# Modulation columns and k weights in blocks of 128 rows at the beginning of an adaLN block

## The chip, the cores and the metric

The kernel runs on one core of a Trainium2 chip. The metric is the device time of one execution in microseconds (us), the median of several runs. A profile of one execution shows when each engine worked: TensorE (PE, with its weight loads as PEld), VectorE (DVE), ScalarE (ACT), GpSimd (POOL) and the queue of SyncE (SP), which issues the transfers.

## What is computed

```python
x = A_x                                            # 2048 x 512, all float32
sa, ca, ga, sb, cb, gb = silu(c) @ w_mod           # six vectors of 512
h = layernorm(x) * (1 + ca) + sa
x = x + ga * linear_attention(h, wqkv, wo)         # 32 heads of 16
h = layernorm(x) * (1 + cb) + sb
x = x + gb * (((h @ w_gate) * (h @ w_up)) @ w_down)
```

The linear attention uses phi(t) = t + 1 above zero and exp(t) below, plus 1e-6, for q and k. Its first sum runs over all 2048 tokens, phi(k) against v, so k of all tokens comes before any output. Products are made in three passes from a high and a low part of each operand (float32r), so one k tile of 128 tokens is four blocks of 128 rows times three matmuls, 12 in all.

## The kernel before

The 2048 tokens are four chunks of four tiles; a tile is 128 tokens by 512 features. The schedule is written out by hand: each engine runs its instructions in the order of the program text, and waits only for data and for buffers. SyncE takes the loads in the order of the text too; a queue of some eight loads is in flight at a time. SBUF tiles come from one pool of 99 buffers, PSUM tiles from two pools of four banks (acc_bank and bank).

At the beginning SyncE loads (lines 122 to 132) the first chunk of x, the vector c, the 512 columns of w_mod for ca as four tiles of 128 x 512, the same for sa, the four row blocks of the k weights, the second chunk of x, the q and v weights and the rest of x.

The work of the beginning (lines 343 to 389) is then:

- keep_on puts filler matmuls on TensorE that keep it busy until data is there. stats, rstd_of, nmr_of and xhat normalise the four tiles of the first chunk (statistics on DVE, a power on POOL, the normalisation on ACT), and transpose_token turns them on TensorE, so that bank k holds 128 features of 512 tokens.
- silu gives the vector sc. mod_acc adds up, on DVE, the four tiles of w_mod, each times a column of sc (lines 159 and 161). mod_col (line 166) adds the result over its 128 partitions on TensorE with a matmul of one moving column for each block of 128 features, and col_out (line 171) brings the column to SBUF. This is done for ca in full, then for sa in full.
- split_raw makes the high part of a weight block on ACT (line 183) and the low part on DVE (line 184). modulated (lines 262 to 273) applies scale and shift to one block of 128 features on ACT, then makes the high part (a cast on DVE with cast, or on ACT) and the low part on DVE.
- product2 (lines 206 to 208) makes k of tiles 0 and 1 block by block; tiles 2 and 3 follow by proj (lines 196 to 198). In between nx, the norm of the second chunk, has its statistics (line 225), variance (233), power (234), nmr (237) and first normalisations (243); k_phi makes phi(k) with two ACT operations and one DVE operation (291, 292, 295), k_split its parts (318, 319).

Behind that stands the loop over 16 tiles. Its first turn makes k of tile 3, normalises the third and the fourth tile of chunk 1 (with k_split_x of tile 1 between them on ACT), runs two of the four column groups of t_tile(0) on TensorE (lines 327 to 329), and then transposes chunk 1 (line 250). The rest of the kernel, with attention and the feed-forward part (line 837 has most of its matmuls), follows that loop.

Of the kernel before, what the change touches and what calls it, by code (L numbers as in the profile page):

```python
# [8 lines left out]
F32 = mybir.dt.float32  # L9
F32R = mybir.dt.float32r  # L10
AF = mybir.ActivationFunctionType
ALU = mybir.AluOpType
AX = mybir.AxisListType

P = 128
# [7 lines left out]
def tile_adaln_block(  # L23
# [12 lines left out]
    nc = tc.nc  # L36
    ctx.enter_context(tc.manual_schedule())
    _, S, D = x.shape
    F = w_gate.shape[1]
    KD = D // P  # L40
# [12 lines left out]
    wqkv_v = wqkv.rearrange("(k p) n -> k p n", p=P)  # L53
# [3 lines left out]
    wm_v = w_mod.rearrange("(p k) n -> p k n", k=KD)  # L57

    pool = lambda name, bufs, **kw: ctx.enter_context(tc.tile_pool(name=name, bufs=bufs, **kw))
    consts = pool("consts", 1)  # L60
# [5 lines left out]
    def f32(ap):  # L66
        return ap.bitcast(F32)
# [3 lines left out]
    def T(p, tag, shape=(P, D), dt=F32, bufs=None):  # L71
        cnt[0] += 1
        return p.tile(list(shape), dt, tag="t" if p is tiles else tag, name=f"{tag}_{cnt[0]}", bufs=bufs)

    def B(tag, shape=(P, D), dt=F32):

        return T(tiles, tag, shape, dt)

    def acc_bank():
        return T(ps_acc, "acc")  # L80

    def bank():
        return T(ps_w, "bank")
# [24 lines left out]
    def load(src, tag):  # L108
        raw = B(tag, (P, *src.shape[1:]))[:src.shape[0]]
        nc.sync.dma_start(raw, src)  # L110
        return raw

    def load_x(ch):
        return [load(xv[ch, j], "x") for j in range(NJ)]

    def load_mod(v):
        return [load(wm_v[:, k, v * D:(v + 1) * D], "raw") for k in range(KD)]

    def load_qkv(n):
        return [load(wqkv_v[k, :, n * D:(n + 1) * D], "raw") for k in range(KD)]  # L120
# [1 line left out]
    xts = [load_x(0)]  # L122
    ct = consts.tile([P, KD], F32, name="ct")
    nc.sync.dma_start(ct, c[0].rearrange("(p k) -> p k", k=KD))
    raw_ca = load_mod(1)
    raw_sa = load_mod(0)
    raw_k = load_qkv(1)
    xts.append(load_x(1))
    raw_q = load_qkv(0)
    raw_v = load_qkv(2)  # L130
# [10 lines left out]
    def keep_on(n):  # L141
        for _ in range(n):
            nc.tensor.matmul(ps_idle, idle[:, :P], idle, start=True, stop=True)
# [3 lines left out]
    sc = consts.tile([P, KD], F32, name="sc")  # L147
# [8 lines left out]
    def mod_acc(acc, raws, ks):  # L156
        for k in ks:
            if k == 0:
                nc.vector.tensor_scalar(acc, raws[k], sc[:, 0:1], None, op0=ALU.mult)
            else:  # L160
                nc.vector.scalar_tensor_tensor(acc, raws[k], sc[:, k:k + 1], acc, op0=ALU.mult, op1=ALU.add)

    def mod_col(acc, ps):

        for b in range(KD):
            nc.tensor.matmul(ps[:, b:b + 1], acc[:, b * P:(b + 1) * P], ones[:, 0:1], start=True, stop=True)
        return ps

    def col_out(v, ps, add):
        t = consts.tile([P, KD], F32, name=f"col{v}")  # L170
        nc.vector.tensor_scalar(t, ps[:, :KD], add, None, op0=ALU.add)
        return t
# [9 lines left out]
    def split(src, h, l, low=None):  # L182
        nc.scalar.activation(h, src, AF.Copy)  # L183
        (low or nc.vector).tensor_tensor(l, src, f32(h), op=ALU.subtract)  # L184

    def split_raw(raw, shape=(P, D), low=None):
        h = B("w", shape, F32R)
        l = B("w", shape, F32R)
        split(raw, h[:raw.shape[0]], l[:raw.shape[0]], low)
        return h, l  # L190
# [6 lines left out]
            nc.tensor.matmul(ps, ah, bl, start=False, stop=False)  # L197
            nc.tensor.matmul(ps, al, bh, start=False, stop=i == n - 1)  # L198

    def product2(pss, pairs):  # L200

        n = len(pairs[0])
        for i in range(n):
            for ps, p in zip(pss, pairs):
                (ah, al), (bh, bl) = p[i]
                nc.tensor.matmul(ps, ah, bh, start=i == 0, stop=False)
                nc.tensor.matmul(ps, ah, bl, start=False, stop=False)
                nc.tensor.matmul(ps, al, bh, start=False, stop=i == n - 1)

    def cut(pair, a, b):  # L210
        return pair[0][:, a:b], pair[1][:, a:b]


    class Norm:
# [25 lines left out]
        def xhat(self, *js):  # L240
            for j in js:
                self.n[j] = B("n")
                nc.scalar.activation(self.n[j], self.tiles[j], AF.Identity,  # L243
                                     scale=self.rstd[:, j:j + 1], bias=self.nmr[:, j:j + 1])

        def transpose(self, *ks):
            for k in ks:
# [31 lines left out]
    wk, wq, wv = [], [], []  # L279
    kx, phk, phq, q_ps = {}, {}, {}, {}  # L280

    def proj(i, w, of=bank):

        ch, j = divmod(i, NJ)
        ps = of()
        product(ps, [(cut(norm[ch].t[k], j * P, (j + 1) * P), w[k]) for k in range(KD)])
        return ps
# [9 lines left out]
    def k_split_x(i):  # L297
        ch, j = divmod(i, NJ)
        kx[i] = [B("xh", dt=F32R), B("xl", dt=F32R)]
        split(norm[ch].n[j], *kx[i])  # L300

    def k_phi(i, ps):
        phi = B("phi")
        phi_a(ps, phi)
        phi_b(ps, phi)
        phk[i] = phi
# [8 lines left out]
    def k_split(i):  # L315
        h, l = B("kh", dt=F32R), B("kl", dt=F32R)
        phi = phk[i]
        nc.scalar.activation(h, phi, AF.Identity, bias=eps_phi)
        nc.vector.scalar_tensor_tensor(l, phi, EPS_PHI, f32(h), op0=ALU.add, op1=ALU.subtract)
        kx[i] += [h, l]  # L320
# [18 lines left out]
    zacc = B("z")  # L339

    n0 = norm[0]
    acc_ca, acc_sa = B("f"), B("f")
    keep_on(20)
    n0.stats(0, 1)
    n0.rstd_of(0, 2)
    n0.stats(2, 3)
    n0.rstd_of(2, 4)
    silu()
    n0.nmr_of(0, 2)
    n0.xhat(0, 1)  # L350
    mod_acc(acc_ca, raw_ca, [0])
    n0.nmr_of(2, 4)
    n0.xhat(2, 3)
    n0.transpose_token(0)
    keep_on(2)
    n0.transpose_token(1)
    keep_on(2)
    n0.transpose_token(2)
    mod_acc(acc_ca, raw_ca, [1, 2, 3])
    keep_on(1)  # L360
    n0.transpose_token(3)
    ps_ca = mod_col(acc_ca, acc_bank())
    mod_acc(acc_sa, raw_sa, [0, 1, 2, 3])
    ca = col_out(1, ps_ca, 1.0)
    keep_on(4)
    ps_sa = mod_col(acc_sa, acc_bank())
    keep_on(9)
    wk.append(split_raw(raw_k[0]))
    sa = col_out(0, ps_sa, 0.0)
    nx = Norm(xts[1])  # L370
    nx.stats(0)
    n0.modulated(ca, sa, 0, cast=nc.vector)
    wk.append(split_raw(raw_k[1]))
    n0.modulated(ca, sa, 1, cast=nc.vector)
    wk.append(split_raw(raw_k[2]))
    n0.modulated(ca, sa, 2)
    nx.stats(1)
    wk.append(split_raw(raw_k[3]))
    n0.modulated(ca, sa, 3)
    ps0, ps1 = acc_bank(), acc_bank()  # L380
    product2((ps0, ps1), [[(cut(n0.t[k], j * P, (j + 1) * P), wk[k]) for k in range(KD)] for j in range(2)])
    nx.stats(2, 3)
    nx.rstd_of()
    k_split_x(0)
    k_phi(0, ps0)
    nx.nmr_of()
    k_phi(1, ps1)
    k_split(0)
    nx.xhat(0, 1)

    tacc = [acc_bank() for _ in range(KD)]
    rows, cols = {}, {}
    accs = {}

    raw_m, raw_o, wo_s = {}, [], []

    def mod_load(*vs):
        raw_m.update({v: load_mod(v) for v in vs})
# [18 lines left out]
             13: lambda: (mod_part(5, 0, 1, 2), cols.update({4: col_out(4, mod_col(accs[4], bank()), 1.0)})),  # L417
             14: lambda: (mod_part(5, 3), wo_s.extend(split_raw(x) for x in raw_o)), 15: lambda: rows.update({5: mod_row(5, accs[5])})}
    q_at = {3: 0, 4: 1, 6: 2, 7: 3}
    ahead = {2: proj(2, wk)}  # L420
    for i in range(NT):
        ch, j = divmod(i, NJ)
        more = ch + 1 < NCH
        if i == 0:
            ahead[3] = proj(3, wk)
        elif i > 1:
            ahead[i + 2] = proj(i + 2, wk) if i + 2 < NT else proj(i + 6 - NT, wq)
        if i in q_at:
            qps = proj(q_at[i], wq)
        if more and j == 0:  # L430
            nx.xhat(2)
        if i + 1 < NT:
            k_split_x(i + 1)
        if more and j == 0:
            nx.xhat(3)
        if i + 1 < NT:
            k_split(i + 1)
        if more and j < 2:
            t_tile(i, 0, 1)
            nx.transpose(2 * j, 2 * j + 1)  # L440
            nx.modulated(ca, sa, 2 * j, 2 * j + 1, cast=nc.vector)
            norm[ch + 1:] = [nx]
        if ch + 2 < NCH and j == 2:
            nx2 = Norm(xts[ch + 2])
            nx2.stats(0, 1)
        if ch + 2 < NCH and j == 3:
            nx = nx2
            nx.stats(2, 3)
            nx.rstd_of()
            nx.nmr_of()  # L450
            nx.xhat(0, 1)
        if i + 2 < NT:
            k_phi(i + 2, ahead.pop(i + 2))
        else:
            q_a(i + 6 - NT, ahead.pop(i + 2))
            q_b(i + 6 - NT)
        if i in q_at:
            q_a(q_at[i], qps)
            q_b(q_at[i])
        if i + 1 < NT:  # L460
            z_add(i + 1)
        if i == NT - 1:
            zps = bank()
            nc.tensor.matmul(zps, ones, zacc, start=True, stop=True)
            zb = consts.tile([P, D], F32, name="zb")
            nc.scalar.activation(zb, zps, AF.Identity, bias=eps_z)
        t_tile(i, *range(2 if more and j < 2 else 0, KD))
        if i in extra:
            extra[i]()
# [61 lines left out]
    ps = proj(6, wq)  # L531
    fs, tt = [], []
    for k in range(KD):
        f = B("n")
# [9 lines left out]
    for g in range(KD):  # L544
        a, b = g * P, (g + 1) * P
# [4 lines left out]
    ps = proj(8, wq)  # L550
# [9 lines left out]
    ps = proj(9, wq)  # L560
# [444 lines left out]
    ps = proj(11, wq)  # L1005
# [177 lines left out]
```

## Time and profile before

| What | Value |
|---|---|
| Median of 3 runs | 572.92 us (571.94 to 573.11) |
| Span of the profiled execution, first to last instruction | 570.9 us |
| TensorE busy | 560.6 us, 98% |
| VectorE busy | 373.8 us, 65% |
| ScalarE busy | 279.7 us, 49% |
| GpSimd busy | 185.6 us, 33% |
| Instructions | 7343 |

For the profiled execution the span is what is known of its own time; it is 2.0 us under the median of the runs. A row of the timeline has the start, the time it took (both in us), the engine, the line in the kernel, the operation, the tiles written and read with their shape, the count, and in brackets the idle time of the engine before it and what ended that. L166 is line 166. Matmuls overlap each other, so their distance is read from the starts. A row of the waits has who waited for whom, the total in us, how often, and the longest. A row of the stage windows has the stretch, its length, the busy time of PE, PEld, DVE, ACT and POOL, the granted TensorE clock (1.00 is full), the busy share of the DMA engines, and GB/s.

### The profile page before, as it was taken

The numbers are of one execution on the slowest core, as the hardware profiler recorded it, in microseconds if no ns is written. First come the engines' busy times: TensorE is split into PE (matmuls) and PEld (weight loads), VectorE is DVE, ScalarE is ACT, GpSimd is POOL, SyncE is SP. The second block draws the span as 40 slices with busy tenths as digits, with TensorE's granted clock in tenths as the row PEclk, the third lists the DMA queues.
The fourth block names the chain that finished last, engine by engine and source line by source line (L and its number), as shares of the span: only waits on it lengthen the run. The fifth ranks groups of instructions, "written<-read, shape, count | busy, mean of one in ns | idle before, by whom it ended". The sixth has DMA issues, their size and how long they took to land.

```text
span 570.9 us, 7343 instructions
## 1 busy us (share of the span) xinstructions
PE 560.6 (98%) x2569; PEld 457.3 (80%) x2569; DVE 373.8 (65%) x613; ACT 279.7 (49%) x500; POOL 185.6 (33%) x191
## 2 busy tenths in 40 slices
PE   7999999999999999999989999999999999999997
PEld 6778888888888778878878888887888888888885
DVE  6876868868768876768776777755554434344444
ACT  3785857546456535445865545533333333334110
POOL 2000000000011300000389666665667446556200
PEclk9999999999999999999999999999999999999999
DMA  8900223302301000804208462699436122100004
GB/s 279 378 6 2 73 75 102 121 0 57 96 0 52 24 1 37 258 0 136 68 2 276 147 209 93 218 337 335 126 110 174 29 56 55 57 18 2 0 1 147
DMA packets 50165, 59.34 MB, mean 104 GB/s; under 512 B 6416, under 2 KB 26896, under 8 KB 50128
## 3 DMA queue, kind: packets, MB, share of 16 engines
q1 hardware_dynamic: 50128, 58.87, 32.0%
q8 instruction: 20, 0.33, 0.2%
q14 instruction: 17, 0.14, 0.1%
HBM read 43.12 MB, written 15.73 MB: 103 GB/s over the span
## 4 chain that ended last, share of the span: by engine, by line
PE 88%; DVE 4%; ACT 2%; DMA 2%; POOL 2%; issue 1%; SPq 0%; POOLq 0%; DVEq 0%; ACTq 0%
PE bank L837 28%; PE acc L614 7%; PE acc L916 6%; PE acc L917 6%; PE acc L918 6%; PE bank L198 5%; PE bank L196 5%; PE bank L197 5%; PE acc L329 3%; PE acc L328 3%; PE acc L327 3%; PE bank L691 2%; PE bank L692 2%; PE bank L690 2%; PE bank L250 1%; PE bank L578 1%
## 5 line engine op out<-in xcount | busy, mean ns | idle before, releaser
L837 PE MATMUL bank<-h,w 128*128 128x512 f32 (+1 forms) x798 | 185.3, 390 | 1.6 <-DVE u L892 1.6
L837 PEld LDWEIGHTS bank<-h,w 128*128 128x128 f32 (+1 forms) x798 | 148.2, 186 | 34.9 <-DVE u L892 2.5
L842 ACT ACTIVATE bank<-bank 128x512 f32<-128x512 f32 (+1 forms) x38 | 22.2, 583 | 144.7 <-PE bank L837 144.7
L677 DVE TENSOR_TENSOR x<-acc,x 128x512 f32<-128x512 f32 x72 | 48.9, 690 | 49.2 <-PE acc L918 48.5
L823 POOL TENSOR_TENSOR w<-raw,w 128x256 fp32r<-128x256 f32 (+3 forms) x38 | 42.2, 1111 | 97.0 <-ACT w L816 76.7
L184 POOL TENSOR_TENSOR w<-raw,w 128x512 fp32r<-128x512 f32 (+1 forms) x25 | 35.5, 1422 | 115.9 <-DVE mv L226 87.5
L916 PE MATMUL acc<-w,kh 128*128 128x512 f32 (+1 forms) x152 | 59.2, 390 | 0.0
L917 PE MATMUL acc<-w,kh 128*128 128x512 f32 (+1 forms) x152 | 59.2, 390 | 0.0
L918 PE MATMUL acc<-w,kl 128*128 128x512 f32 (+1 forms) x152 | 59.1, 389 | 0.0
L234 POOL TENSOR_TENSOR rstd<-ve,half 128x4 f32<-128x4 f32 (+1 forms) x9 | 9.4, 1045 | 138.2 <-DVE ve L233 136.6
L184 DVE TENSOR_TENSOR kl<-u,kh 128x512 fp32r<-128x512 f32 (+1 forms) x38 | 27.4, 761 | 34.5 <-ACT kh L183 32.6
L823 POOL TENSOR_TENSOR w<-t,w 128x512 fp32r<-128x512 f32 (+1 forms) x38 | 48.0, 1286 | 0.0
L196 PE MATMUL bank<-w,h 128*128 128x512 f32 x112 | 44.9, 401 | 0.0
L198 PE MATMUL bank<-w,h 128*128 128x512 f32 x112 | 43.9, 392 | 0.0
L197 PE MATMUL bank<-w,h 128*128 128x512 f32 x112 | 43.6, 389 | 0.0
L614 PE MATMUL acc<-w,xh 128*128 128x512 f32 x120 | 38.1, 398 | 0.0
L916 PEld LDWEIGHTS acc<-w,kh 128*128 128x128 f32 (+1 forms) x152 | 28.5, 188 | 6.0
L918 PEld LDWEIGHTS acc<-w,kl 128*128 128x128 f32 (+1 forms) x152 | 28.5, 188 | 6.0
L917 PEld LDWEIGHTS acc<-w,kh 128*128 128x128 f32 (+1 forms) x152 | 28.5, 188 | 6.0
L243 ACT ACTIVATE n<-x,nmr,rstd 128x512 f32<-128x512 f32 x32 | 24.1, 805 | 17.2 <-DVE nmr L237 17.2
L892 DVE TENSOR_TENSOR u<-bank,u 128x512 f32<-128x512 f32 (+1 forms) x19 | 13.1, 691 | 28.8 <-PE bank L837 28.8
L183 ACT ACTIVATE w<-raw 128x512 fp32r<-128x512 f32 (+2 forms) x44 | 26.4, 618 | 3.2 <-DMA raw<-in_A_wqkv_dram 2.2
(177 smaller groups left out, 1098.1 us busy)
## 6 DMA issues: line engine op xcount, KB each, us to landing
raw<-in_w_mod_dram SPq DMA_DIRECT2D x24, 256.0 KB, 3.7
raw<-in_B_w_down_dram SPq DMA_DIRECT2D x20, 256.0 KB, 3.0
raw<-in_B_w_gate_dram SPq DMA_DIRECT2D x36, 128.0 KB, 3.5
raw<-in_B_w_up_dram SPq DMA_DIRECT2D x36, 128.0 KB, 3.6
x<-in_A_x_dram SPq DMA_DIRECT2D x16, 256.0 KB, 5.4
kept<-f SPq DMA_DIRECT2D x16, 256.0 KB, 2.1
f<-kept SPq DMA_DIRECT2D x16, 256.0 KB, 4.6
side_s<-h SPq DMA_DIRECT2D x16, 256.0 KB, 2.9
```

The source lines that it names most:

```text
L183: nc.scalar.activation(h, src, AF.Copy)
L184: (low or nc.vector).tensor_tensor(l, src, f32(h), op=ALU.subtract)
L196: nc.tensor.matmul(ps, ah, bh, start=i == 0, stop=False)
L197: nc.tensor.matmul(ps, ah, bl, start=False, stop=False)
L198: nc.tensor.matmul(ps, al, bh, start=False, stop=i == n - 1)
L614: nc.tensor.matmul(yps[i], x, y, start=False, stop=k == KD - 1 and x is al, skip_group_check=True)
L677: nc.vector.tensor_tensor(xt, dn[j], xt, op=ALU.add)
L823: sub = lambda out, x, y: (on or nc.gpsimd).tensor_tensor(out, x, f32(y), op=ALU.subtract)
L837: mm = lambda x, y, **kw: nc.tensor.matmul(ps, x[:, k], y, skip_group_check=True, **kw)
L916: nc.tensor.matmul(dn[j], hh[:, a:b], dh[:n], start=i == 0, stop=False)
L917: nc.tensor.matmul(dn[j], hh[:, a:b], dl[:n], start=False, stop=False)
L918: nc.tensor.matmul(dn[j], hl[:, a:b], dh[:n], start=False, stop=i == len(hs) - 1)
```

## The change

The loads of w_mod for ca and sa are cut by feature blocks in place of the rows: one load now has all 512 input rows of 128 columns (128 partitions x 4 x 128), and the order is ca block b, sa block b, k rows block b, for b = 0 to 3. The sums of mod_acc at the beginning are gone: mod_block(b) makes both columns of a block on TensorE from the loaded tiles, four accumulated matmuls for each, and mod_out(b) brings both to SBUF in one DVE operation. The fourth tile of the first chunk is normalised on DVE. k of the first four tiles is made in four PSUM banks, block by block between the column blocks, so that proj for tiles 2 and 3 disappears. The order of the next chunk's statistics against k_phi and k_split changes, and ten fillers go.

```diff
-    raw_ca = load_mod(1)
-    raw_sa = load_mod(0)
-    raw_k = load_qkv(1)
+    raw_m, raw_k = {}, []
+    for b in range(KD):
+        for v in (1, 0):
+            raw_m[v, b] = load(wm_v[:, :, v * D + b * P:v * D + (b + 1) * P], "raw")
+        raw_k.append(load(wqkv_v[b, :, D:2 * D], "raw"))
     xts.append(load_x(1))
...
+        def xhat_on(self, engine, *js):
+            for j in js:
+                self.n[j] = B("n")
+                engine.tensor_scalar(self.n[j], self.tiles[j], self.mv[:, j, 0:1], self.rstd[:, j:j + 1],
+                                     op0=ALU.subtract, op1=ALU.mult)
...
-    acc_ca, acc_sa = B("f"), B("f")
+    add = consts.tile([P, 2], F32, name="add")
+    nc.gpsimd.memset(add[:, 0:1], 1.0)
+    nc.gpsimd.memset(add[:, 1:2], 0.0)
+    mod = consts.tile([P, 2, KD], F32, name="mod")
+    ca, sa = mod[:, 0], mod[:, 1]
+    ps_mod = acc_bank()[:, :2 * KD].rearrange("p (v b) -> p v b", v=2)
+
+    def mod_block(b):
+        for i, v in enumerate((1, 0)):
+            raw = raw_m.pop((v, b))
+            for k in range(KD):
+                nc.tensor.matmul(ps_mod[:, i, b:b + 1], raw[:, k], sc[:, k:k + 1], start=k == 0, stop=k == KD - 1)
+
+    def mod_out(b):
+        nc.vector.tensor_tensor(mod[:, :, b], ps_mod[:, :, b], add, op=ALU.add)
+
+    def block_in(b):
+        n0.modulated(ca, sa, b, cast=nc.vector)
+
+    def w_in(b):
+        wk.append(split_raw(raw_k[b]))
+
     keep_on(20)
     n0.stats(0, 1)
     n0.rstd_of(0, 2)
-    n0.stats(2, 3)
+    n0.stats(2)
+    n0.nmr_of(0, 2)
+    n0.xhat(0)
+    n0.stats(3)
     n0.rstd_of(2, 4)
     silu()
-    n0.nmr_of(0, 2)
-    n0.xhat(0, 1)
-    mod_acc(acc_ca, raw_ca, [0])
-    n0.nmr_of(2, 4)
-    n0.xhat(2, 3)
+    n0.xhat(1)
+    n0.nmr_of(2, 3)
+    n0.xhat(2)
+    n0.xhat_on(nc.vector, 3)
     n0.transpose_token(0)
     keep_on(2)
     n0.transpose_token(1)
     keep_on(2)
+    mod_block(0)
+    n0.transpose_token(3)
     n0.transpose_token(2)
-    mod_acc(acc_ca, raw_ca, [1, 2, 3])
-    keep_on(1)
-    n0.transpose_token(3)
-    ps_ca = mod_col(acc_ca, acc_bank())
-    mod_acc(acc_sa, raw_sa, [0, 1, 2, 3])
-    ca = col_out(1, ps_ca, 1.0)
+    mod_out(0)
     keep_on(4)
-    ps_sa = mod_col(acc_sa, acc_bank())
-    keep_on(9)
-    wk.append(split_raw(raw_k[0]))
-    sa = col_out(0, ps_sa, 0.0)
+    w_in(0)
+    block_in(0)
+    k_ps = [acc_bank(), acc_bank(), bank(), bank()]
+
+    def k_block(b, *js):
+        for j in js:
+            (hh, hl), (wh, wl) = cut(n0.t[b], j * P, (j + 1) * P), wk[b]
+            nc.tensor.matmul(k_ps[j], hh, wh, start=b == 0, stop=False)
+            nc.tensor.matmul(k_ps[j], hh, wl, start=False, stop=False)
+            nc.tensor.matmul(k_ps[j], hl, wh, start=False, stop=b == KD - 1)
+
+    k_block(0, 0, 1)
+    mod_block(1)
+    w_in(1)
+    mod_out(1)
+    k_block(0, 2)
+    block_in(1)
+    k_block(0, 3)
+    k_block(1, 0, 1)
+    mod_block(2)
+    w_in(2)
+    k_split_x(0)
+    mod_out(2)
     nx = Norm(xts[1])
     nx.stats(0)
-    n0.modulated(ca, sa, 0, cast=nc.vector)
-    wk.append(split_raw(raw_k[1]))
-    n0.modulated(ca, sa, 1, cast=nc.vector)
-    wk.append(split_raw(raw_k[2]))
-    n0.modulated(ca, sa, 2)
+    k_block(1, 2)
+    mod_block(3)
+    block_in(2)
+    w_in(3)
+    mod_out(3)
+    k_block(1, 3)
+    block_in(3)
+    k_block(2, 0)
+    k_block(3, 0)
     nx.stats(1)
-    wk.append(split_raw(raw_k[3]))
-    n0.modulated(ca, sa, 3)
-    ps0, ps1 = acc_bank(), acc_bank()
-    product2((ps0, ps1), [[(cut(n0.t[k], j * P, (j + 1) * P), wk[k]) for k in range(KD)] for j in range(2)])
-    nx.stats(2, 3)
+    k_phi(0, k_ps[0])
+    k_block(2, 1)
+    k_block(3, 1)
+    nx.stats(2)
+    k_split(0)
+    k_phi(1, k_ps[1])
+    nx.stats(3)
     nx.rstd_of()
-    k_split_x(0)
-    k_phi(0, ps0)
+    k_block(2, 2, 3)
+    k_block(3, 2, 3)
     nx.nmr_of()
-    k_phi(1, ps1)
-    k_split(0)
     nx.xhat(0, 1)
...
-    ahead = {2: proj(2, wk)}
+    ahead = {2: k_ps[2], 3: k_ps[3]}
     for i in range(NT):
         ch, j = divmod(i, NJ)
         more = ch + 1 < NCH
-        if i == 0:
-            ahead[3] = proj(3, wk)
-        elif i > 1:
+        if i > 1:
```

More of the change, by code (lines that the diff above doesn't have):

```diff
@@ L198, in product @@
             nc.tensor.matmul(ps, al, bh, start=False, stop=i == n - 1)
[L200 to L208, printed above, removed]
     def cut(pair, a, b):
@@ L393, in tile_adaln_block @@
     accs = {}
-    raw_m, raw_o, wo_s = {}, [], []
+    raw_o, wo_s = [], []
     def mod_load(*vs):
```

## The prediction

> **What bounds the kernel now.** I read four views: the page for the span and the chain that ended last, the waits of TensorE over the whole span, the timeline of the first 45 us, and the stage windows for the clock and the transfers.
>
> ```profile
> span 570.9 us, 7343 instructions
> PE 88%; DVE 4%; ACT 2%; DMA 2%; POOL 2%; issue 1%; SPq 0%; POOLq 0%; DVEq 0%; ACTq 0%
> ```
>
> ```profile
> PE bank L257 <- ACT n L243: 1.6, 1, 1.6
> PE bank L837 <- DVE u L892: 1.6, 2, 1.5
> ```
>
> The chain is TensorE for 88% of the span. The longest waits of its matmuls once data is in are 1.6 us in total each, one of them at the very beginning (L257, the first transposes) and one in the last part (L837). So whatever moves TensorE's steady work later or earlier at the beginning moves the end by about the same amount: nothing behind it is idle enough to absorb it. The change touches only the beginning, so I look at when TensorE gets into its steady sequence. The mark I use is the first transposes of the second chunk (L250), because everything behind them has the same order before and after.
>
> ```profile
> 16.37 0.78 ACT L262 ACTIVATE f<-bank,col,col 128x512 f32<-128x512 f32 x1 [1.25 <-DVE col L171]
> ...
> 18.47 0.50 PE L206 MATMUL acc<-w,h 128*128 128x512 f32 x1 [0.18 <-DVE h L270]
> ...
> 24.08 0.50 PE L208 MATMUL acc<-w,h 128*128 128x512 f32 x1
> ...
> 24.62 0.60 ACT L291 ACTIVATE phi<-acc 128x512 f32<-128x512 f32 x1 [2.04 <-PE acc L208]
> 25.25 0.63 ACT L292 ACTIVATE phi<-phi 128x512 f32<-128x512 f32 x1
> 25.67 0.17 DVE L233 TENSOR_SCALAR ve<-mv 128x4 f32<-128x4 f32 x1
> 25.92 1.38 POOL L234 TENSOR_TENSOR rstd<-ve,half 128x4 f32<-128x4 f32 x1 [16.11 <-DVE ve L233]
> 26.35 0.68 DVE L295 SCALAR_TENSOR_TENSOR phi<-acc,phi 128x512 f32<-128x512 f32 x1
> 27.07 0.72 ACT L318 ACTIVATE kh<-phi,eps_phi 128x512 fp32r<-128x512 f32 x1
> 27.70 2.21 ACT L243 ACTIVATE n<-x,nmr,rstd 128x512 f32<-128x512 f32 x3
> 29.82 0.62 ACT L183 ACTIVATE xh<-n 128x512 fp32r<-128x512 f32 x1
> 30.34 0.80 ACT L243 ACTIVATE n<-x,nmr,rstd 128x512 f32<-128x512 f32 x1
> ```
>
> ```profile
> 30.60 0.39 PE L327 MATMUL acc<-kh,xh 128*128 128x512 f32 x1
> ...
> 31.96 1.04 PE L250 MATMUL bank<-ident,n 128*128 128x128 f32 x8
> ```
>
> The reader is to see two strands that meet at 31.96. One is TensorE: the first k tile complete at 24.58, two more products, six matmuls of L327 to L329 from 30.60 (1.36 us, 0.227 each), then the transposes. The other is the second chunk's norm: its variance line L233 at 25.67, the power on POOL, and four normalisations on ACT, the last over at 31.14. It is 0.8 us early, so it costs nothing. It is early because L233 stands **ahead** of the k features on DVE: 25.67 against 26.35 for the first of them.
>
> **The change part by part.** The columns first. Each goes from sums on DVE and one reduction per column to four accumulated products per column, eight in a block of 128 rows. The nearest row is the reduction itself, the same shapes, 128x128 weights and one moving column:
>
> ```profile
> 13.20 0.95 PE L166 MATMUL acc<-ones,f 128*128 128x1 f32 x8
> ```
>
> Four calls are eight passes in 0.95 us, of which the last ends 0.25 late: 0.10 us a pass. mod_block is eight calls, sixteen passes, 1.66 us; four blocks are 6.6 us of TensorE in place of 1.9 for both columns. As bounds I take half of that pass (0.05) and one and a half (0.15). [...]
>
> What this buys is DVE: eight operations of L159 and L161 go. The transfers:
>
> ```profile
> 7.66 0.70 DVE L225 BATCH_NORM_STATS2 st<-x 128x6 f32<-128x512 f32 x1 [0.39 <-DMA x<-in_A_x_dram]
> ```
>
> ```profile
> 10.00:11.00 1.00, 0.77 (x6) 0.73 (x7) 0.96 (x3) 1.00 (x3) 0.00 (x0) 1.00 1.07 412
> ```
>
> ```profile
> 140.00:142.00 2.00, 2.00 (x20) 1.96 (x18) 1.63 (x4) 1.09 (x2) 0.00 (x0) 1.00 1.03 292
> ```
>
> ```profile
> raw<-in_B_w_gate_dram SPq DMA_DIRECT2D x2, 256.0 KB, 3.9
> ```
>
> The new w_mod loads have rows of 512 bytes, as the w_gate loads at 140 us: 292 GB/s in place of 412 (the last number of a window row), 0.9 us a load in place of some 0.65. From the fourth tile of x at 7.66 on: columns of block 0 at about 10.0, its k rows at 10.6, and so on every 2.4 us; block 3's columns at 17.3, its k rows at 18.0. SP issues as many DMAs as before in the same place, and the second chunk of x slips by some 1.5 us, to 18.6 to 20.7. All of this turns out early against what follows, so the transfers cost nothing, and the cover is 6 us in block 3.
>
> Now the queues, each instruction at the later of its engine's turn and its inputs, and some 0.05 us from one engine to the next (24.58 to 24.62 above).
>
> ```profile
> 2.00 6.60 PE L143 MATMUL acc<-w 128*128 128x512 f32 x20 [2.00 <-DVE w L138]
> 6.58 0.71 POOL L234 TENSOR_TENSOR rstd<-ve,half 128x2 f32<-128x2 f32 x1 [3.91 <-DVE ve L233]
> ...
> 11.19 0.60 PE L257 MATMUL bank<-ident,n 128*128 128x128 f32 x4
> 12.09 0.60 PE L257 MATMUL bank<-ident,n 128*128 128x128 f32 x4
> ...
> 18.02 0.40 DVE L270 CAST h<-f 128x512 fp32r<-128x512 f32 x1
> 18.45 0.69 DVE L273 TENSOR_TENSOR h<-f,h 128x512 fp32r<-128x512 f32 x1
> ...
> 24.76 0.66 DVE L225 BATCH_NORM_STATS2 st<-x 128x6 f32<-128x512 f32 x1
> 25.45 0.18 DVE L226 BATCH_NORM_AGGREGATE mv<-st 128x2 f32<-128x6 f32 x1
> ```
>
> *Start.* The first rstd is there at 7.29, so xhat(0) starts at 7.45. The fillers end at 8.60; two groups of transposes with two fillers each, 0.95 a group by the starts of L257, bring TensorE to 10.5. xhat on DVE for the fourth token is bounded by nothing and by the 0.80 that ACT takes for the same tile; even with that it is over by 10.8, ahead of its transposes, so it costs nothing. The two new memsets on POOL fall into its idle time before L234 (3.91 us). mod_block(0) runs 10.5 to 12.2, two groups of transposes to 13.0, the modulated tile f0 on ACT 13.0 to 13.8 (0.78), the cast 0.42: first k product at 14.3 in place of 18.47. That is the gain.
>
> *Blocks 0 to 2.* Six products to 15.95 (with 0.3 waiting for the low part). Behind them mod_block(1), whose loads landed long ago, to 17.6; only then can mod_out(1), f1 (18.0 to 18.8) and the next cast run. This wait of DVE on mod_out is new, and behind it in DVE's queue stand the next cast, its low part and the split's low part, for which TensorE then waits. Tile 3's product waits 0.55 for the bank that f1 reads; block 1's six products end at 20.95, mod_block(2) at 22.6, three products, mod_block(3) at 24.95. On DVE mod_out(3) stands behind statistics of the next chunk, h2, its low part and a split, and comes at 25.5; f3 25.7 to 26.5, cast 27.0, low part 27.7. **Tile 0 is complete at 28.2**, against 24.58: three blocks' 5.0 us of columns and a round trip TensorE, DVE, ACT, DVE for each take back the early start.
>
> ```profile
> 50.95 1.01 POOL L234 TENSOR_TENSOR rstd<-ve,half 128x4 f32<-128x4 f32 x1 [23.65 <-DVE ve L233]
> ```
>
> *Behind tile 0.* The last statistics of the next chunk, with L233, now stand **behind** k_phi(1) on DVE. From 28.2: Relu 0.62, Exp 0.68, phi 0.73 (tile 0); kh 0.63; Relu 0.62, Exp 0.68, phi 0.60 (tile 1); statistics 0.92; variance 0.22; the power 1.25 (its two rows have 1.38 and 1.01); nmr 0.21, like the variance; three normalisations at 0.70, a copy 0.53, the fourth 0.83: 10.7 us with the 0.05 that lead in. Transposes at **38.8**, against 31.96: 6.9 late.
>
> TensorE meanwhile has 18 products and 6 matmuls of the first t tile, 24 at 0.227, and is through at about 33.5. It waits 5.3 us, and all that is behind the transposes waits with it. The same arithmetic on the order of before gives 31.9 where the row has 31.96.
>
> *The clock.* What such a wait costs beside itself:
>
> ```profile
> 566.44 0.39 PE L918 MATMUL acc<-w,kl 128*128 128x512 f32 x1
> ```
>
> ```profile
> 568.00:569.00 1.00, 0.00 (x0) 0.00 (x0) 0.00 (x0) 0.00 (x0) 0.00 (x0) 1.00 0.57 217
> 569.00:570.00 1.00, 0.00 (x0) 0.00 (x0) 0.00 (x0) 0.00 (x0) 0.00 (x0) 0.53 0.12 45
> ```
>
> After the last matmul (over at 566.83) the granted clock, the third number from the end, falls to half within the slice from 569.0: by its mean 0.53 at about 569.1, after 2.2 us. So a wait of 5.3 us should bring half clock. Coming back is shown by the first 20 fillers: 6.60 us where 20 at 0.227 would take 4.7, a loss of 1.9. Some of it falls into a stall that is there anyway:
>
> ```profile
> 39.22 0.40 PE L196 MATMUL bank<-w,h 128*128 128x512 f32 x1
> ...
> 41.15 0.40 PE L327 MATMUL acc<-kh,xh 128*128 128x512 f32 x1
> ```
>
> Six products in 1.93 where 1.36 would do: 0.6 to spare. I add 1.2 (bounds 0 and 2.1). [...]
>
> **The sum** is 6.9 + 1.2 = 8.1 us on the profiled span of 570.9, so 579.0. The median of the runs is 572.92, 2.0 above the span; with the same 2.0 the forecast is 581.0. By half the price of a pass (0.05) the sum is 2.5 smaller, by one and a half (0.15) 2.5 larger.
>
> **The rivals.** *The clock holds* through the wait, as it did through the 1.6 us of L257: 572.9 + 6.9 = 579.8. [...] *The clock falls earlier*, between 10 and 26 us, because a pass moves one column and counts as little work: another 1.9 us of lost speed on the path, about 583; against it, TensorE is never idle for more than 0.7 us there, and the gap of 1.6 us at L257 did no harm. *The other side:* tile 0's path doesn't run through the column passes, because they fall into TensorE's waits and the loads set the pace. Then block 3 ends with its columns at 17.3, mod_out, f3, cast and low part 2.6 later, tile 0 complete at 20.4, transposes 10.7 behind it at 31.1: 0.9 earlier, 572.0. It decides from 21.3 on (31.96 less 10.7); the queue order, with mod_block(b) behind products that wait for block b-1's tile, speaks against it, and even passes that cost nothing leave the round trips (tile 0 at 23.8, 2.6 slower). *The change doesn't do what it says:* transfers in rows of 512 bytes so slow that every block waits for its columns; that needs 1.6 us a load in place of 0.9, and would add to the loss.
>
> **How the numbers follow.** Forecast 0.60; clock holds 0.20; cheap passes 0.06; earlier fall 0.07; the other side 0.05; slow transfers 0.02. The range takes in the clock case, cheap passes down to 0.06 and the upper bounds of clock and passes in part: 578.0 to 583.5. About 0.2% (1.1 us) is what a measurement can tell from no change. Faster by more than that 0.04, within it 0.03, slower 0.93, since only the other side and what I have not seen lie below.
>
> **What would show it.** In the changed profile: L166's successor passes at 0.10 us; first k product near 14.3; idle time of ACT and DVE ended by column passes; tile 0's Relu near 28.2; variance L233 near 33.7; the transposes L250 near 38.8 with some 5 us of TensorE idle before them, released by ACT n; granted clock near 0.5 behind them for some 4 us. I am wrong if tile 0 is complete before 21.3, or if L233 runs ahead of the k features.

## The result, and the profile after

The changed kernel takes **582.27 us** (580.95 to 583.34, five runs), beside 571.98 us (571.85 to 573.11, five runs) for the kernel before: a ratio of 1.0175, interval 1.0161 to 1.019. It is slower, as forecast, and inside the range; the forecast of 581.0 is 1.3 low. The profiled execution has a span of 580.1 us where the one before had 570.9: 9.2 more, against 8.1 in the sum. The medians are 10.3 apart, since the two profiled executions are not the median ones: 580.1 is 0.5 under the median span of the changed kernel (580.6), and 570.9 is some 0.6 above that of the kernel before (its median time less the 1.7 that lies between time and span in the runs that list both). What follows explains the 9.2.

The timeline of the changed kernel shows the steps of the prediction. L351 are the column passes, L354 mod_out, L391 to L393 the k products, L260 modulated, L289 the Relu of phi, L225 to L229 the second chunk's variance, power and nmr, L235 its normalisation, L248 its transposes (the old L250), L325 to L327 t_tile.

```profile
10.84 1.84 PE L351 MATMUL acc<-sc,raw 128*128 128x1 f32 x16
...
14.62 0.51 PE L391 MATMUL acc<-w,h 128*128 128x512 f32 x1
...
16.36 1.84 PE L351 MATMUL acc<-sc,raw 128*128 128x1 f32 x16
...
18.24 0.16 DVE L354 TENSOR_TENSOR mod<-acc,add 128x2 f32<-128x2 f32 x1 [2.35 <-PE acc L351]
18.44 0.78 ACT L260 ACTIVATE f<-bank,mod 128x512 f32<-128x512 f32 x1 [3.81 <-DVE mod L354]
...
28.80 0.60 ACT L289 ACTIVATE phi<-acc 128x512 f32<-128x512 f32 x1 [1.78 <-PE acc L393]
...
33.84 0.39 PE L327 MATMUL acc<-kl,xh 128*128 128x512 f32 x1
...
34.27 0.17 DVE L225 TENSOR_SCALAR ve<-mv 128x4 f32<-128x4 f32 x1
...
35.76 2.22 ACT L235 ACTIVATE n<-x,nmr,rstd 128x512 f32<-128x512 f32 x3 [3.07 <-DVE nmr L229]
36.62 0.33 PE L248 MATMUL bank<-ident,n 128*128 128x128 f32 x1 [2.39 <-ACT n L235]
...
39.26 1.33 PE L248 MATMUL bank<-ident,n 128*128 128x128 f32 x5 [0.75 <-ACT n L235]
...
40.24 0.78 PE L325 MATMUL acc<-kh,xh 128*128 128x512 f32 x1
```

The reader is to see the two delays one behind the other. The first product is early (14.62, before 18.47), but each further block waits for its columns: DVE for TensorE (2.35 us), then ACT for DVE (3.81 us). Tile 0 is complete at 28.76 in place of 24.58. Then the second chunk's variance, now queued behind the k features, comes at 34.27 in place of 25.67; TensorE has run out of matmuls at 34.23, and its idle time is ended by ACT's normalised tiles. The waits of 8 to 50 us say the same in four rows (who waits for whom, total, how often, longest):

```profile
ACT f L260 <- DVE mod L354: 8.5, 3, 3.8
DVE mod L354 <- PE acc L351: 6.8, 3, 2.7
ACT n L235 <- DVE nmr L229: 5.7, 3, 3.1
...
PE bank L248 <- ACT n L235: 3.9, 4, 2.4
```

The stage windows of the same execution show the clock (third number from the end) and the rate of the transfers (last number):

```profile
14.00:16.00 2.00, 1.93 (x8) 0.98 (x7) 1.72 (x3) 0.63 (x2) 0.00 (x0) 1.00 1.16 322
16.00:18.00 2.00, 2.00 (x19) 1.92 (x17) 0.00 (x0) 0.00 (x0) 0.00 (x0) 1.00 1.05 384
...
36.00:38.00 2.00, 0.66 (x2) 0.28 (x2) 0.00 (x0) 2.00 (x4) 0.00 (x0) 0.95 0.00 0
38.00:40.00 2.00, 1.22 (x5) 0.93 (x6) 0.84 (x2) 2.00 (x4) 0.00 (x0) 0.50 0.00 0
...
42.00:44.00 2.00, 2.00 (x6) 1.52 (x5) 1.97 (x5) 2.00 (x4) 0.00 (x0) 0.50 0.00 0
44.00:46.00 2.00, 2.00 (x14) 1.68 (x13) 1.80 (x3) 0.45 (x2) 0.00 (x0) 0.84 0.00 0
```

The slices show 1.00, 0.50 and means in between; if the clock is either full or half, a 2 us slice with a mean of m has 4(1 - m) us of half clock in it. So by this estimate it is at half for 0.2 us of the slice at 36, all of 38 to 44, and 0.64 us of the slice at 44: 6.84 us, from 37.8 to 44.64.

How far the delay is carried is read from the same matmuls in both traces. First the kernel before, then the changed one:

```profile
32.75 0.47 PE L327 MATMUL acc<-kh,xh 128*128 128x512 f32 x1
...
35.60 1.03 PE L250 MATMUL bank<-ident,n 128*128 128x128 f32 x8
...
58.86 1.03 PE L250 MATMUL bank<-ident,n 128*128 128x128 f32 x8
...
537.88 0.39 PE L918 MATMUL acc<-w,kl 128*128 128x512 f32 x1
```

```profile
45.12 1.04 PE L248 MATMUL bank<-ident,n 128*128 128x128 f32 x8
...
67.80 1.04 PE L248 MATMUL bank<-ident,n 128*128 128x128 f32 x8
...
547.04 0.39 PE L957 MATMUL acc<-w,kl 128*128 128x512 f32 x1
```

With 40.24 from the first fence, the changed kernel is 7.5 us late when t_tile goes on, 9.5 late at the next transposes (the half clock), 8.9 late at 58.86, and 9.2 late at 537.88. Behind that stage 0.6 is given back and 0.2 lost again; nothing absorbs the rest.

### The profile page after: what moved, and what is told of

Its sections match the earlier page's. It is cut to its first block, busy times and chain, and to the rows that moved or that the text cites. A ratio compares the mean times of both kernels' runs of the same rounds, so it can differ in the third digit from the quotient of the medians.

```text
span 580.1 us, 7412 instructions
## 1 busy us (share of the span) xinstructions
PE 567.2 (98%) x2607; PEld 463.6 (80%) x2607; DVE 370.9 (64%) x610; ACT 277.9 (48%) x497; POOL 184.2 (32%) x193
## 4 chain that ended last, share of the span: by engine, by line
PE 90%; DVE 4%; ACT 3%; DMA 1%; issue 1%; POOL 0%; DVEq 0%; SPq 0%; ACTq 0%
PE bank L876 29%; PE acc L653 7%; PE acc L955 6%; PE acc L956 6%; PE acc L957 6%; PE bank L198 4%; PE bank L199 4%; PE bank L200 4%; PE acc L325 3%; PE acc L327 3%; PE acc L326 3%; PE bank L730 2%; PE bank L731 2%; PE bank L729 2%; PE bank L248 1%; PE acc L145 1%
## 5 line engine op out<-in xcount | busy, mean ns | idle before, releaser
L881 ACT ACTIVATE bank<-bank 128x512 f32<-128x512 f32 (+1 forms) x38 | 22.2, 583 | 145.0 <-PE bank L876 144.9
L198 PE MATMUL bank<-w,h 128*128 128x512 f32 x104 | 41.7, 401 | 0.0
L200 PE MATMUL bank<-w,h 128*128 128x512 f32 x104 | 40.6, 390 | 0.0
L199 PE MATMUL bank<-w,h 128*128 128x512 f32 x104 | 40.5, 389 | 0.0
L235 ACT ACTIVATE n<-x,nmr,rstd 128x512 f32<-128x512 f32 x31 | 23.6, 805 | 21.6 <-DVE nmr L229 21.6
L325 PE MATMUL acc<-kh,xh 128*128 128x512 f32 x64 | 26.8, 419 | 0.0
```

The source lines that it names most:

```text
L325: nc.tensor.matmul(tacc[k], xh[:, a:b], kh, start=first, stop=False)
```

## The experiments

**Theory:** two delays in series, the columns' passes and round trips ahead of tile 0 (some 4 us), and the second chunk's norm queued behind the k features on VectorE (some 3 us more until TensorE restarts); then half clock. **Rivals:** the loads in rows of 512 bytes set the pace; the half clock is most of the loss. From the version with both edits on there is one theory more (theory 4), drawn from the runs up to there: the column passes do not hold the clock, fillers do. Where executions of one kernel differ, their mean granted clock over the span is given. A stretch of 3.42 us at half clock (the length is that of the windows below) lowers it by 0.003, so by an estimate 0.994 is two such stretches, 0.988 four; the profile of the changed kernel has 6.84 us of half clock at 0.994, that of the version with the columns early 13.7 us at 0.988.

**The norm first.** The changed kernel with the second chunk's norm ahead of the k features, as in the kernel before:

```diff
-    nx.stats(1)
+    nx.stats(1, 2, 3)
+    nx.rstd_of()
     k_phi(0, k_ps[0])
...
-    nx.stats(2)
-    k_split(0)
+    nx.nmr_of()
     k_phi(1, k_ps[1])
-    nx.stats(3)
-    nx.rstd_of()
+    k_split(0)
```

> The second chunk's statistics, variance and nmr go back ahead of the k features, all else as in the changed kernel. Theory 1 (two delays in series: tile 0 complete 4.1 us later because the column passes lie on its path, and behind it the norm of the second chunk that waits for the k features; then half clock): tile 0 stays at 28.7, the variance line comes at about 30.8 in place of 34.27, the last transposes of the second chunk at 36.1 in place of 40, TensorE waits some 1 us and the clock stays at full: 4.2 us over the kernel before, 576. Rival 2 (the loads in rows of 512 bytes pace everything): no change from the changed kernel, 582. Rival 3 (half clock is most of the loss and a matter of the beginning, not of the wait): half clock and about 581 still.

577.6 us, ratio 1.0093 (1.0057 to 1.0128). Its timeline:

```profile
28.76 0.60 ACT L289 ACTIVATE phi<-acc 128x512 f32<-128x512 f32 x1 [1.78 <-PE acc L393]
...
30.61 0.17 DVE L225 TENSOR_SCALAR ve<-mv 128x4 f32<-128x4 f32 x1
...
35.61 0.76 PE L248 MATMUL bank<-ident,n 128*128 128x128 f32 x5 [0.77 <-ACT n L235]
...
36.13 0.47 PE L325 MATMUL acc<-kh,xh 128*128 128x512 f32 x1
```

Tile 0 stands where it stood; the variance is 3.7 us earlier and t_tile goes on 4.1 earlier (36.13 for 40.24), 3.4 behind the kernel before. The clock stays full in this execution, whose span is 574.6: 5.5 less than the changed kernel's. So between the profiled executions the order on VectorE and the half clock that follows it are 5.5 of the 9.2 us, and the delay of tile 0 is what is left. By the medians they are 4.7 of 10.3. The four spans are 574.6 and 573.8 at a clock of 0.999, 577.2 at 0.994, 577.9 at 0.989: in two of the executions the clock fell somewhere else.

**Fillers in the wait.** Twenty matmuls on idle data ahead of the second chunk's first transposes, so that TensorE is busy while it waits:

```diff
+                for _ in range(fill if k == ks[0] else 0):
+                    nc.tensor.matmul(ps, idle[:, :P], idle, start=True, stop=True)
...
-            nx.transpose(2 * j, 2 * j + 1)
+            nx.transpose(2 * j, 2 * j + 1, fill=20 if i == 0 else 0)
```

> 20 filler matmuls stand between the first t tile's columns and the transposes of the second chunk, so that TensorE is busy while it waits. Theory 1: transposes at the same time as in the changed kernel, end near 39.7, granted clock 1.00 throughout, 1.0 to 2.2 us faster than the changed kernel, so 7.0 to 8.0 us over the kernel before: 579 to 580. Rival 3 (half clock is most of the loss): over 5 us faster, 577 or less. If the clock falls all the same, the fillers don't count as work.

581.56 us, 1.0147 (1.0108 to 1.0186). The spans fall into two groups: 577.2 and 578.3 at 0.999, and 581.4 and 581.5 at 0.991 and 0.994. The first pair is what was expected: 6.6 and 7.7 above the 570.6 that the kernel before typically has, by the delay alone. The profile caught one of the other pair. Its windows:

```profile
18.00:20.00 2.00, 1.74 (x6) 1.12 (x5) 1.12 (x4) 1.82 (x3) 0.00 (x0) 0.79 1.07 391
20.00:22.00 2.00, 2.00 (x6) 1.52 (x6) 1.22 (x3) 0.00 (x0) 0.00 (x0) 0.50 1.04 382
22.00:24.00 2.00, 2.00 (x16) 1.84 (x15) 0.00 (x0) 0.00 (x0) 0.00 (x0) 0.85 1.05 384
...
26.00:28.00 2.00, 2.00 (x10) 2.00 (x10) 1.44 (x3) 0.02 (x2) 0.00 (x0) 0.50 1.06 390
...
32.00:34.00 2.00, 2.00 (x8) 1.60 (x7) 0.87 (x2) 1.21 (x3) 0.00 (x0) 0.79 0.00 0
34.00:36.00 2.00, 2.00 (x10) 1.68 (x9) 1.51 (x4) 1.70 (x3) 0.00 (x0) 1.00 0.01 4
```

The fillers keep the clock full from 34 on, but it falls where no theory had it: for 3.44 us from 19.16 and 6.84 us from 26.0, in the stage of the column passes, with TensorE shown as busy 1.74 to 2.00 of 2.00. That is what the prediction's rival "the clock falls earlier" says, and the reason for the later experiments on it.

**One product in place of four** in blocks 1 to 3, so that a block has four passes and not sixteen (the kernel then leaves three of the four products out of each sum):

```diff
-            for k in range(KD):
+            n = KD if b == 0 else 1
+            for k in range(n):
```

> Blocks 1 to 3 make their columns from one of the four accumulated products (four passes in place of sixteen a block); the other three products are left out of the sum, the loads stay. Theory 1: the passes lie on the path of tile 0, so it is complete at about 26.1 in place of 28.7, and the transposes come 2.5 earlier, with the same wait and the same half clock in front: 6.1 us over the kernel before, 578 to 580. Rival 2 (the loads pace it): tile 0 stays at 28.7, no change. A rival with passes hidden in TensorE's waits gives no change either.

577.85 us, 1.0101 (1.0081 to 1.012), all four executions at 0.994. Its tile 0:

```profile
25.55 0.60 ACT L289 ACTIVATE phi<-acc 128x512 f32<-128x512 f32 x1 [1.77 <-PE acc L394]
```

Tile 0 is 3.25 us earlier with the same loads, for 36 passes fewer (3.8 us at 0.106), and the range of the spans (575.7 to 577.3) lies 3.3 to 3.5 under the 579.2 to 580.6 that the changed kernel has at the same clock. The passes set the pace of the blocks; the rival with the loads falls. The two stretches of half clock in this profile are at the wait and, for 3.4 us, from 25.6 on, behind a slice (22 to 24) in which TensorE is busy for only 0.84 of 2.00 us. So fewer passes alone do not keep the clock up.

**The columns early:** the passes of block 1 take the place of four fillers, and those of blocks 2 and 3 come one block earlier. No block was to wait for its columns any more.

```diff
-    keep_on(4)
+    mod_block(1)
...
-    mod_block(1)
+    mod_block(2)
...
-    mod_block(2)
+    mod_block(3)
...
-    mod_block(3)
```

> The column passes of block 1 take the place of the four fillers, those of blocks 2 and 3 stand one block earlier; the same number of passes, the norm of the second chunk still behind the k features. Theory 1: the round trips fall away and one block's passes take a place that fillers held: tile 0 complete at 25.5 in place of 28.7, the last transposes at 36.8 in place of 40, half clock still: 5.4 us over the kernel before, 577.5 to 579. Rival 2 (the loads pace it): TensorE now waits for columns that have not landed, tile 0 near 28, no gain.

A miss: 583.06 us, 1.0205 (1.017 to 1.024), no faster than the changed kernel itself, with clocks of 0.988 and 0.982 in all executions. Tile 0's Relu starts at 30.01, not at 25.5. There are two reasons. The first is that the waits did not go:

```profile
12.53 1.84 PE L351 MATMUL acc<-sc,raw 128*128 128x1 f32 x16
...
15.70 1.84 PE L351 MATMUL acc<-sc,raw 128*128 128x1 f32 x16
...
17.58 0.16 DVE L354 TENSOR_TENSOR mod<-acc,add 128x2 f32<-128x2 f32 x1 [2.62 <-PE acc L351]
...
22.35 1.84 PE L351 MATMUL acc<-sc,raw 128*128 128x1 f32 x16
...
24.23 0.16 DVE L354 TENSOR_TENSOR mod<-acc,add 128x2 f32<-128x2 f32 x1 [3.29 <-PE acc L351]
```

The passes of block 1 are those at 12.53, but mod_out(1) starts at 17.58, when the passes of block 2 are over, and VectorE has waited 2.62 us; mod_out(2) waits in the same way for the passes of block 3. Those passes now stand ahead of it in the text and write the same PSUM tile, which may be why; no run tells. So this edit does not test what the round trips cost. The second reason is the clock: the windows have half clock from 18.7 to 22.2, from 29.0 to 32.4 and from 39.2 for 6.84 us, 13.7 in all, where the changed kernel's profile has 6.84. The passes are closer together and four fillers fewer. Both edits together (**early and first**):

> Both earlier edits at once: column passes early, and the second chunk's norm ahead of the k features. Theory 1 with full clock: tile 0 complete at 25.5, last transposes at 32.8, 0.9 us over the kernel before, 573. [...] If the loads set the pace: 580 or more.

578.86 us, 1.0131 (1.0099 to 1.0162). The profiled execution has a clock of 0.985 and a span of 582.0, with half clock from 14.6 to 28.3 and for 3.4 us more from 35.1; the other three have 0.993 and 577.1. The time was forecast at 575 to 576.5 with a fall of the clock and near 573 without. Beside the norm first alone (577.6) the early columns bring nothing. With **four fillers behind the passes of each of blocks 1 to 3**, otherwise the same:

```diff
     mod_block(2)
+    keep_on(4)
...
     mod_block(3)
+    keep_on(4)
```

(and one such line behind block 1's passes.)

> The same with four filler matmuls behind the passes of each of the blocks 1, 2 and 3. The fillers cost 2.8 us of TensorE on the path: with full clock 3.7 us over the kernel before, 575.7. Theory 4 (passes alone let the clock fall, fillers among them hold it): clock 0.999 in every execution, a narrow spread around 575.7, though the kernel has 12 matmuls more. Rival (the clock's fall has nothing to do with the passes): the same low clocks as without the fillers, and 2.8 us more than there.

577.93 us, 1.0105 (1.0079 to 1.0131). Three of four executions hold the full clock, at spans of 575.4 to 576.3; one has 0.992 and 579.6, where the theory had the full clock in all. Though there are twelve more matmuls (2.7 us at 0.227), these three spans are under all four without the fillers (577.1 and more), since the clock stays up; the intervals of the two ratios overlap. The time was forecast 2 us too low: even at full clock tile 0's Relu starts at 30.07, where 25.5 and the fillers would have given 28.2, since mod_out of blocks 1 and 2 still comes behind the next block's passes (at 19.11 and 24.58). At full clock the version with the norm first alone is still shorter (573.8 and 574.6).

**The passes in the kernel before.** The direct test: two runs of fillers, four and nine matmuls, replaced by 10 and 20 passes of one moving column (each call makes two), which take about as long at full clock (3.2 us at 0.106 for 2.95 at 0.227).

```diff
-    keep_on(4)
+    passes(5, acc_ca)
...
-    keep_on(9)
+    passes(10, acc_ca)
```

> The kernel before, with the fillers between its columns (four and nine matmuls of 512 columns) replaced by column passes on the same tiles (10 and 20 passes of one column, results unused); TensorE is occupied as long as before, 1.0 and 2.1 us, and the first k product starts at 18.5 as before. Theory 4: the clock falls for 3 to 7 us near 18 to 20 us in some or all executions, clock 0.994 or less there and 1 to 3 us slower than the kernel before; executions without a fall equal it. Rival (passes hold the clock as fillers do): clock 0.999 and 572 in all.

575.18 us, 1.0045 (1.0029 to 1.006), with a clock of 0.993 or 0.994 in four of four; the 17 executions of the kernel before beside it have 0.998 to 1.0 (one of seven in an earlier group had 0.995). The timeline and the windows of this kernel:

```profile
13.73 1.25 PE L148 MATMUL acc<-ones,f 128*128 128x1 f32 x10
...
15.74 4.12 PE L148 MATMUL acc<-ones,f 128*128 128x1 f32 x20
```

```profile
16.00:18.00 2.00, 2.00 (x11) 2.00 (x12) 0.99 (x4) 1.88 (x4) 0.00 (x0) 0.52 1.05 358
18.00:20.00 2.00, 2.00 (x10) 2.00 (x11) 1.93 (x5) 2.00 (x5) 0.00 (x0) 0.50 1.05 389
20.00:22.00 2.00, 2.00 (x5) 1.53 (x5) 2.00 (x4) 2.00 (x4) 0.00 (x0) 0.50 1.08 403
22.00:24.00 2.00, 2.00 (x8) 1.62 (x7) 1.97 (x5) 0.32 (x1) 0.00 (x0) 0.78 1.02 370
```

TensorE is busy throughout and the clock is at half for 6.8 us from 16.1 on, in which the 20 passes take 4.12 us, 0.2 each. In the same four slices the kernel before, with its fillers, has 1.00. So the matmuls of 512 columns were not there to fill time alone: these passes of one column did not hold the clock.

**The kernel before with the norm behind.** Could the later norm be of use where tile 0 is early? The kernel before, with the second chunk's statistics behind all of block 3, its fourth tile normalised on VectorE, and the low parts of the q weights on GpSimd:

```diff
+    nx = Norm(xts[1])
+    nx.stats(0, 1, 2, 3)
...
+    nx.xhat_on(nc.vector, 3)
...
-             1: lambda: (wq.extend(split_raw(r) for r in raw_q[1:2]),),
+             1: lambda: (wq.extend(split_raw(r, low=nc.gpsimd) for r in raw_q[1:2]),),
```

> The kernel before with three moves on the path that the traces showed: the second chunk's first statistics behind the first chunk's blocks on VectorE (so that these end 1.2 us sooner), its fourth normalisation on VectorE ahead of the second tile's k feature, and the low parts of the q weights on GpSimd. Theory 1: tile 0 complete at 23.3 in place of 24.6, the transposes at 30.7 in place of 32.0, and 0.6 less waiting in the second turn: 1.4 us faster than the kernel before, 570.5. Rival (VectorE is hidden there anyway): no change, 572.

572.96 us, 1.0008 (0.9999 to 1.0017): the same. The transposes start at 30.42, 1.5 us earlier, but the timeline shows what came in their place:

```profile
30.42 1.03 PE L256 MATMUL bank<-ident,n 128*128 128x128 f32 x8
...
34.26 1.28 POOL L184 TENSOR_TENSOR w<-raw,w 128x512 fp32r<-128x512 f32 x1 [6.89 <-ACT w L183]
34.60 1.48 DVE L316 TENSOR_TENSOR z<-phi,phi 128x512 f32<-128x512 f32 x1
...
37.66 0.69 DVE L279 TENSOR_TENSOR h<-f,h 128x512 fp32r<-128x512 f32 x1
...
38.53 1.30 POOL L184 TENSOR_TENSOR w<-raw,w 128x512 fp32r<-128x512 f32 x1 [3.00 <-ACT w L183]
38.73 1.66 DVE L279 TENSOR_TENSOR h<-f,h 128x512 fp32r<-128x512 f32 x1
...
40.44 0.50 PE L198 MATMUL bank<-w,h 128*128 128x512 f32 x1 [0.95 <-DVE h L279]
```

The same VectorE instruction takes 0.69 us alone and 1.66 beside GpSimd's, and TensorE waits for it. Without the GpSimd part:

> The kernel before with the second chunk's statistics behind the whole of block 3 and its fourth normalised tile on VectorE, as in the experiment with the norm behind, but with the low parts of wq left where the kernel before has them, so that GpSimd runs nothing beside VectorE's features. Theory (GpSimd's instructions beside VectorE's, 0.68 us stretched to 1.48 to 1.69, gave the gain back): VectorE's instructions of the second chunk take 0.68 us all along, and the time is some 0.8 us under the kernel before, 571.2 to 571.6 where that is 572.0 to 572.4. Rival (what the second chunk gains is absorbed further on in any case): the same as before within 0.3 us.

571.61 us (11 runs) beside 572.25 (15 runs), 0.9994 (0.9985 to 1.0003). From 28 to 48 us GpSimd runs nothing there, and L279 takes 0.69 us at the same place:

```profile
30.45 1.04 PE L256 MATMUL bank<-ident,n 128*128 128x128 f32 x8
...
38.55 0.69 DVE L279 TENSOR_TENSOR h<-f,h 128x512 fp32r<-128x512 f32 x1
```

The median is at the edge of what the theory gave (571.2 to 571.6), but its interval takes in no change, so no version here is shown to beat the kernel before. In its profile the third chunk's transposes are still 1.5 us earlier (57.33 for 58.86) and the last L918 at the end of the same stretch of matmuls 1.1 (536.74 for 537.88); but its span of 569.7 is also the shortest of the kernel before in that group.

## Why the prediction was right, and where it was not

- **The price of a pass** was 0.10 us; the passes at 16.36 and the product behind them at 18.06 are 1.70 apart: 0.106 each. The range and a chance of 0.06 take in passes at 0.06 us; no run shows that price: it is 0.106 here and 0.10 at L166 in the kernel before.
- **The start and blocks 0 to 2.** First product forecast at 14.3, measured 14.62; tile 0 at 28.2, measured 28.76. The waits ran where the queue order put them. "The other side", with tile 0 by 21.3, is out: with 36 passes fewer (3.8 us) tile 0 came 3.25 us earlier.
- **Behind tile 0.** Variance forecast at 33.7, measured 34.27; TensorE out of work at 33.5, measured 34.23. The wait was to last 5.3 us and took 5.0, from 34.23 to the last five transposes at 39.26; three single transposes ran in it as their tiles came. t_tile goes on 7.5 us late where the step had 6.9; most of the difference is already half clock, as the next point but one shows.
- **The transfers** cost nothing, as forecast: 322 GB/s while the 512-byte rows are under way and 384 behind them, and no wait of TensorE in this stage is ended by a load. Longer rows in the changed kernel were not tried by themselves.
- **The clock** is the term that was mis-sized. The sum had 1.2 us, from "some 4 us" of half clock; the trace has 6.84 us. From the last five transposes to t_tile it takes 0.98 us (39.26 to 40.24), where the version with the norm first takes 0.52 at full clock (35.61 to 36.13): 0.46 of the 7.5 is half clock, and the delay itself is 7.0. The twelve matmuls behind make 7.5 into 9.5. Of that 0.6 is given back, as forecast, and 0.2 lost again further on. So the half clock cost 2.1 at the end, 0.9 more than its term, at the upper bound that the prediction gave it; with 0.1 more on the delay that is the 1.1 by which the sum was short on the span. The prediction read the price of coming back off the first 20 fillers; the windows of the kernel before have a granted clock of 1.00 there (2 to 8 us), so no row shows those 1.9 us as half clock.
- **The stretches of half clock** last 3.44, 6.84 and 13.7 us in these profiles: one, two and four times 3.42. No run shows why. The fall at 37.8 is 3.6 us behind the end of TensorE's work (34.23), with two single transposes in between (36.62 and 37.33). Nor is there one idle time that brings the fall: in the kernel before it came 2.2 us behind the last matmul (over at 566.83), and in the changed kernel's profile the clock stays at 1.00 for 4.0 us behind the last matmul (over at 575.99).
- **The rival "the clock falls earlier"** had a chance of 0.07, and the reason against it ("TensorE is never idle for more than 0.7 us there") was wrong. Time busy alone did not hold the clock: with the fillers in the wait it fell to 0.50 at 26.0, in the stage of the passes, and TensorE is shown as busy for 2.00 of 2.00 us in every slice from 22 to 32. The profiled execution happens to have only the fall at the wait. Two of its five executions have clocks of 0.991 and 0.988, by the estimate above one and two stretches more, at spans of 581.5 and 581.6; where these lie wasn't profiled, but their times, 583.18 and 583.34, are what the rival gave (about 583). In the version with both edits, three stretches more by the same estimate (clocks of 0.985 and 0.993) cost 4.9 us (582.0 against 577.1), 1.6 each.
- **"The clock holds"** gave 579.8. The two executions with fillers and a clock of 0.999 took 578.9 and 580.0, so that price was right, but nothing in the changed kernel holds it.

What stays open: how many columns a matmul needs to hold the clock; why the stretches have their length; why one execution falls early and the next doesn't; and what the round trips cost beside the passes, since no run takes them away.

## What to carry to other kernels

Before a sum is moved from VectorE to TensorE, count its passes at their measured price (0.106 us here, with 16 weight loads for the 16 passes of a block), and see which queue then waits for the result: here VectorE, busy for 65% of the span, was relieved and TensorE, busy for 98%, got some 5 us more of passes, with a round trip through three engines per block. An instruction that feeds TensorE next (the norm) belongs ahead of work that is needed later. When passes are moved earlier to end a wait, look in the trace whether the wait is gone. Where the granted clock dips, ask how many columns the matmuls of that stage move (in the kernel before, passes of one column had 0.50 where fillers of 512 had 1.00), and judge a kernel by several executions with their clocks.

## What was not expected of the hardware

- TensorE that the profile shows as busy can lose its clock: 30 passes of one column in place of 13 matmuls of 512, in the kernel before, brought it to half for 6.8 us in the profiled execution, and the other three have the same mean clock.
- In these profiles half clock comes in pieces of 3.42 us (3.44, 6.84, 13.7), so an execution's mean clock gives an estimate of their number (0.994 at 6.84 us, 0.988 at 13.7).
- Two VectorE instructions were stretched beside GpSimd's: L279, 0.69 us alone, took 1.66 beside one of 1.30, and L316, 0.68 us without the GpSimd part, took 1.48 beside one of 1.28. That is 0.97 and 0.80 us more, most of the 1.10 and 0.94 us that GpSimd's had left to run when they started. Why, no run shows.
